# Reordering the first chunks of an FNet and gated-MLP kernel: one early high part moved up, the statistics and norms of four rows spread over more chunks

## The chip, the cores and the metric

The kernel runs on one core of a Trainium2 chip. The metric is the device time of one execution in microseconds. A core has several engines that run their own instruction streams in program order and wait for each other through semaphores: TensorE (PE in the profile, with its weight loads shown apart as PEld), VectorE (DVE), ScalarE (ACT), GpSimd (POOL) and SyncE (SP), which here only issues transfers between the device memory and the on-chip memory. Transfers are carried out by 16 DMA engines.

## The reference

The kernel computes one transformer-like block on x, 2048 rows of 512. Only the first lines matter here:

```python
x = A_x
mod = (_silu(c) @ w_mod).reshape(c.shape[0], 6, 1, -1)
sa, ca, ga, sb, cb, gb = ...
h = _layernorm(x, axis=-1) * (1 + ca) + sa
x = x + ga * _A_ref(h, A_dft_seq_re, A_dft_seq_im, A_dft_hid_re, A_dft_hid_im)
h = _layernorm(x, axis=-1) * (1 + cb) + sb
x = x + gb * _B_ref(h, B_w_in, B_w_sp, B_b_sp, B_w_out)
```

`_A_ref` is a Fourier mixing: y = C_re (h D_re^T) - C_im (h D_im^T), with C the two 2048 x 2048 sequence matrices and D the two 512 x 512 hidden matrices. The kernel multiplies by the sequence matrices first, so its first work is G = C_re x' and C_im x', with x' the plainly normalised x; scale and shift are folded into later matrices. `_B_ref` is a gated MLP with a 2048 x 2048 spatial matrix. All data are 32-bit floats.

## The kernel before, in words

Every product is made from three matmuls on operands split in two: a high part, which is the value rounded to TensorE's 32-bit format, and a low part, the difference between the value and the high part. ACT makes high parts (a copy into the other type), DVE makes low parts (a subtraction). The three products high-high, high-low and low-high are summed in PSUM.

The first stage, `mm_a` (L513), goes through *chunks* n = 0 to 127. A chunk takes one tile of a sequence matrix, 128 x 512, and one *row* of x', that is 128 of its rows by 512 columns, and does twelve matmuls of 128 x 128 by 128 x 512: four column groups k, three products each. The helper `matmul3` has its three matmuls on L96, L97 and L98; the first six chunks have their own order, all from L524: first the four with both high parts, then the four with the tile's low part, then the four with the row's low part.

Which tile and row a chunk takes at the start: chunks 0 and 1 use row 0, 2 and 3 row 1, 4 row 2, 5 row 3, 6 row 2, 7 row 3 (the list `PAIRED`). From chunk 8 on four rows at a time are used: rows 4 to 7 in chunks 8 to 11 and again in 12 to 15, rows 8 to 11 from chunk 16. So each new row has a latest time.

A tile of a sequence matrix goes through these steps, each of which is an instruction:

- it is a quarter of a block, which SyncE loads (`load` L165, `load_block` L152, `load_half` L157). Two blocks are held. A block's successor is loaded when its last quarter has been turned (inside `prep_hi`);
- `prep_hi(n)` (L252): DVE transposes 32 x 32 squares (`squares`, L190 in the profile, tile `t`), then ACT copies it into the high part `ah` (L269);
- `prep_lo(n)` (L279): DVE subtracts, giving the low part `al` (L290).

A row of x goes through these:

- SyncE loads four rows to a tile (`load_x`, L425);
- statistics: `stats_x` (L436, by `norm` and `stats`) puts two operations on DVE (mean and variance, L104 and L106) and three small ones on POOL (L108, L109, L116), whose results are the norm's scale and bias. Rows 0 to 3 use `stats_first` (L439), with three operations on DVE (L442, L444, L445) and two on POOL (L446, L447);
- `norm_x` (L486): ACT applies scale and bias (L120), tile `xn`; all but the first column, which is one in x' and is set by a POOL memset (L491 for rows above 3);
- `hi_h` (L498): ACT copies it in another order into the high part `hh` (L500). Rows 0 to 3 use `hi_first` (L460), which makes `hh` straight from x (L463) with a one-column copy behind it (L469);
- `lo_h` (L502): DVE subtracts, giving `hl` (L505).

The order of all this is written by hand, and each engine follows it. A prologue of plain calls does the first steps. After it, the loop over n calls `prep(n)`, which is `prep_hi(n + 3)` and `prep_lo(n + 2)` unless these have been done, then `mm_a(n)`, then `run(n)`. `run(n)` calls what `at(n, f, ...)` has hung on chunk n, in the order in which the `at` calls were made. A chunk's number there thus places an instruction in each engine's stream, and every instruction behind it on the same engine waits with it.

Other streams in this stretch: SyncE's loads in order are the blocks, rows of x, the vector c (`load_row`) and parts of w_mod (`load_columns`). Eight semaphores serve the transfers in turn, so each issue waits for the landing of an earlier one.

Of the kernel before, what the change touches and what calls it, by code (L numbers as in the profile page):

```python
# [19 lines left out]
def fnet_gmlp_kernel(  # L20
# [103 lines left out]
    def at(n, f, *a):  # L124
        fill.setdefault(n, []).append((f, a))
# [31 lines left out]
    def load_half(tile_, a, h, engs=(nc.sync,) * 4):  # L157

        v = a.rearrange("(b j) (a s) -> a j b s", j=32, a=4)
        for q in range(4):  # L160
            engs[q].dma_start(tile_[32 * q:32 * q + 32], v[q][:, :, 64 * h:64 * h + 64])
# [3 lines left out]
    def load(b):  # L165
        if b < len(src):
            stage[b] = blocks.tile([P, 16, P], F32, tag="stage", bufs=2, name=f"stage{b}")
            load_block(stage[b], src[b])
        elif b < len(src) + 2:
            j = b - len(src)  # L170
            XB.append(blocks.tile([P, 4, Q], F32, tag="stage", bufs=2, name=f"xb{j}"))
            for g in range(2):
                nc.sync.dma_start(XB[j][:, 2 * g:2 * g + 2], ht_d[g].rearrange("(k p) t -> p k t", p=P)[:, 2 * j:2 * j + 2])
                for kk in range(2):
                    TT[2 * j + kk, g] = XB[j][:, 2 * g + kk]
        elif 4 * (b - NB0) < NE - N4:
            i, gh = divmod(b - NB0, NQ)
            g, h = divmod(gh, 2)
            p = PROD[i]
            stage[b] = blocks.tile([P, 2, 16, 64], F32, tag="stage", bufs=2, name=f"stage{b}")  # L180
            for r in range(2):
                load_half(stage[b][:, r], s_d[S_OF[p], r, g] if p in S_OF else
                          quad(w_sp, r + (2 if p == 4 else 0), g + (2 if p == 1 else 0)), h)
# [5 lines left out]
    def squares(dst, block, k):  # L189
        nc.vector.transpose(dst.rearrange("p (b i) -> p b i", i=32), block[:, :, 32 * k:32 * k + 32])  # L190
# [10 lines left out]
    def slot(i, name, dtype=F32):  # L201
        return slots[0].tile([P, Q], dtype, tag=f"slot{i}", bufs=1, name=name)
# [19 lines left out]
    def form_t(n):  # L222

        if n < N1:
            gg, p, kk = (n - N2) // 4, (n - N2) // 2 % 2, n % 2
            return TT[2 * p + kk, gg]
        p = YPROD[(n - N1) // 4 % len(YPROD)]
        gg, kk = divmod(n % 4, 2)
        a, b, c, d = TT[kk, gg], TT[2 + kk, gg], TT[kk, 2 + gg], TT[2 + kk, 2 + gg]
        return {6: S2[gg, kk], 7: a if n < N3 else c, 4: b if n < N3 else d, 5: c if n < N3 else a, 3: d if n < N3 else b}[p]  # L230
# [21 lines left out]
    def prep_hi(n):  # L252
        if n >= NE or n in highs:
            return
        highs.add(n)
        if N2 <= n < N4:
            T[n] = form_t(n)
        else:
            b, k = PAIRED[n] if n < 8 else divmod(n, 4) if n < N2 else (NB0 + (n - N4) // 4, (n - N4) % 4)
            if b != NB0:  # L260
                T[n] = blocks.tile([P, Q], F32, tag="t", bufs=2, name=f"t{n}")
            if b == NB0:
                assert n in T
            elif n >= N4:
                squares(T[n], stage[b][:, k % 2], k // 2)
            else:
                squares(T[n], stage[b], k)
        AH[n] = SE[2][:, n - N4] if N4 <= n < N4 + 4 else blocks.tile([P, Q], F32R, tag="ah", bufs=4, name=f"ah{n}")
        nc.scalar.activation(AH[n], T[n], AF.Copy)  # L269
        if not N2 <= n < N4 and k == 3:  # L270
            done = stage.pop(b)
            if b == 0:
                stage[2] = done
                load_half(done[:, :, 64:], src[2], 1)
            elif b != NB0:
                load(b + 2)


    def prep_lo(n):  # L279
        if n >= NE or n in lows:  # L280
            return
        lows.add(n)
        if N2 <= n < N4 and n % 4 == 3:
            AL[n] = slot(0, f"al{n}", F32R) if slots else zrow[0].tile([P, Q], F32R, tag="z1u", bufs=6, name=f"al{n}")
        elif N4 <= n < N4 + 4:
            AL[n] = slot(9 + n - N4, f"al{n}", F32R)
        else:
            AL[n] = blocks.tile([P, Q], F32R, tag="al", bufs=3, name=f"al{n}")
        t = T.pop(n)
        nc.vector.tensor_tensor(AL[n], t, AH[n].bitcast(F32), op=ALU.subtract)  # L290
# [148 lines left out]
    def stats_first(s):  # L439

        m = spool.tile([P, 12], F32, tag="first", bufs=4, name=f"first{s}")
        nc.vector.bn_stats(m[:, :6], X[s])  # L442
        mv = m[:, 8:]
        nc.vector.bn_aggr(mv[:, :2], m[:, :6])  # L444
        nc.vector.tensor_scalar(mv[:, 1:2], mv[:, 1:2], EPS, None, op0=ALU.add)  # L445
        nc.gpsimd.tensor_tensor(mv[:, 2:3], mv[:, 1:2], mhalf, op=ALU.pow)  # L446
        nc.gpsimd.tensor_scalar(mv[:, 3:4], mv[:, 0:1], mv[:, 2:3], -1.0, op0=ALU.mult, op1=ALU.mult)  # L447
        NRM[s] = mv[:, 2:3], mv[:, 3:4]
# [11 lines left out]
    def hi_first(s):  # L460
        h_hi[s] = hpool.tile([P, ND, P], F32R, name=f"hh{s}")
        h = h_hi[s].rearrange("p k (a i) -> p k a i", i=32)
        nc.scalar.activation(h, X[s].rearrange("p (a k i) -> p k a i", a=4, i=32), AF.Identity,  # L463
                             bias=NRM[s][1], scale=NRM[s][0])
        if s:
            one_first(s)

    def one_first(s):
        nc.scalar.activation(h_hi[s][:, 0, :1], ones[:, :1], AF.Copy)  # L469
# [608 lines left out]
    prep_hi(1)  # L1078
    stats_first(1)
    prep_lo(1)  # L1080
    hi_first(1)
    prep_hi(2)
    load_half(stage[0][:, :, :64], src[2], 0)
    stats_first(2)
    norm_x(1)
# [9 lines left out]
    at(1, lo_h, 2)  # L1095
    at(2, hi_first, 3)
    at(2, norm_x, 3)
    at(2, prep_lo, 5)
    at(3, lo_h, 3)
    at(3, prep_lo, 6)  # L1100
    at(0, load_x, 1, range(2, 4))
    at(2, load_row)
    at(9, silu_row)
# [3 lines left out]
    at(12, load_columns, 0)  # L1107
    at(19, load_ht, 0)
    at(28, load_ht, 1)
    for s, n in ((4, 3), (5, 3), (6, 6), (7, 6), (8, 10), (9, 10)):  # L1110
        m = n + (s == 9)
        at(n, stats_x, s)
        at(m + 1, norm_x, s)
        at(m + 2, hi_h, s)
        at(m + 3, lo_h, s)
# [19 lines left out]
    for j, turn, weigh, row, fold, hi in ((0, (25, 26, 27, 28), (29, 29, 30, 30), 26, (34, 34, 35, 36), (40, 37, 38, 39)),  # L1135
# [8 lines left out]
        n = weigh[3] + 1  # L1144
# [20 lines left out]
    for t in range(NQ):  # L1165
        n = 8 * NQ * (t + 1)
# [136 lines left out]
    for i, p in enumerate(PROD):  # L1303
        for k in range(8):
            n = NB[p] + 2 * k
# [11 lines left out]
    for f in range(NF):  # L1317
        n = N4 + 24 + 8 * f
# [109 lines left out]
```

## Time and profile before

| what | value |
|---|---|
| median of three runs | 933.23 us (933.17 to 933.29) |
| profiled execution | 933.75 us, its span from first to last instruction 932.0 us |
| TensorE busy | 924.7 us, 4053 matmuls |
| VectorE, ScalarE, GpSimd busy | 737.6, 409.3 and 198.3 us |
| granted TensorE clock | 1.000 |

Times in the timeline are from the start of the span. A row of the timeline has the start, the duration, the engine, the line, the operation, what is written from what is read, the shape and how many instructions are merged; in brackets stands how long the engine had been idle and what ended that, as far as semaphores tell. TensorE's matmuls overlap, so the time of one is best read from the distance between starts. For DVE and ACT too, the next instruction can start before the end shown of the one ahead of it.

### The profile page before, as it was taken

The numbers are of one execution on the slowest core, as the hardware profiler recorded it, in microseconds if no ns is written. First come the engines' busy times: TensorE is split into PE (matmuls) and PEld (weight loads), VectorE is DVE, ScalarE is ACT, GpSimd is POOL, SyncE is SP. The second block draws the span as 40 slices with busy tenths as digits, with TensorE's granted clock in tenths as the row PEclk, the third lists the DMA queues.
The fourth block names the chain that finished last, engine by engine and source line by source line (L and its number), as shares of the span: only waits on it lengthen the run. The fifth ranks groups of instructions, "written<-read, shape, count | busy, mean of one in ns | idle before, by whom it ended". The sixth has DMA issues, their size and how long they took to land.

```text
span 932.0 us, 12356 instructions
## 1 busy us (share of the span) xinstructions
PE 924.7 (99%) x4053; PEld 760.3 (82%) x4053; DVE 737.6 (79%) x1217; ACT 409.3 (44%) x734; POOL 198.3 (21%) x376
## 2 busy tenths in 40 slices
PE   8999999999999999999999999999999999999998
PEld 6788888888888888888888888888888888888886
DVE  6889967788687677875669788899799789896762
ACT  5685434233132321322577877674544544331221
POOL 1330000224654165323512320331000000000000
PEclk9999999999999999999999999999999999999999
DMA  9996762856639977996463864444464556744551
GB/s 215 202 225 132 154 155 50 192 147 161 164 84 308 302 210 220 273 331 245 128 224 135 271 208 103 114 107 106 105 145 103 132 140 138 176 100 151 187 175 57
DMA packets 251200, 157.88 MB, mean 169 GB/s; under 512 B 148704, under 2 KB 218592, under 8 KB 251008
## 3 DMA queue, kind: packets, MB, share of 16 engines
q1 hardware_dynamic: 236512, 119.44, 51.7%
q0 software_dynamic: 12272, 36.86, 11.4%
q10 hardware_dynamic: 2352, 0.79, 0.3%
q8 instruction: 32, 0.52, 0.3%
q14 instruction: 32, 0.26, 0.1%
HBM read 120.33 MB, written 36.71 MB: 169 GB/s over the span
## 4 chain that ended last, share of the span: by engine, by line
PE 94%; DMA 2%; DVE 1%; SPq 1%; issue 1%; ACT 0%; ACTq 0%; DVEq 0%
PE gp L98 12%; PE gp L97 11%; PE gp L96 11%; PE gw L98 9%; PE gw L97 9%; PE gw L96 9%; PE yp L98 3%; PE yp L97 3%; PE yp L96 3%; PE op L98 3%; PE op L96 3%; PE op L97 3%; PE fp L98 1%; PE fp L96 1%; PE fp L97 1%; PE z2s L98 1%
## 5 line engine op out<-in xcount | busy, mean ns | idle before, releaser
L269 ACT ACTIVATE ah<-t 128x512 fp32r<-128x512 f32 x236 | 149.0, 631 | 364.7 <-DVE t L190 259.1
L290 DVE TENSOR_TENSOR al<-t,ah 128x512 fp32r<-128x512 f32 x236 | 161.0, 682 | 54.9 <-PE gp L97 25.1
L97 PE MATMUL gp<-al,hh 128*128 128x512 f32 x488 | 190.1, 390 | 0.6 <-DVE al L290 0.6
L98 PE MATMUL gp<-ah,hl 128*128 128x512 f32 x488 | 190.0, 389 | 0.1
L96 PE MATMUL gp<-ah,hh 128*128 128x512 f32 x488 | 190.0, 389 | 0.0
L190 DVE STREAM_TRANSPOSE t<-stage 128x512 f32<-128x512 f32 x236 | 165.7, 702 | 9.6 <-DMA stage<-in_A_dft_seq_re_dram 4.7
L97 PE MATMUL gw<-al,bh 128*128 128x512 f32 x400 | 155.6, 389 | 0.0
L98 PE MATMUL gw<-ah,bl 128*128 128x512 f32 x384 | 149.6, 390 | 0.1
L96 PE MATMUL gw<-ah,bh 128*128 128x512 f32 x384 | 149.4, 389 | 0.0
L97 PEld LDWEIGHTS gp<-al,hh 128*128 128x128 f32 x488 | 91.6, 188 | 20.6 <-DVE al L290 1.6
L98 PEld LDWEIGHTS gp<-ah,hl 128*128 128x128 f32 x488 | 91.6, 188 | 19.4 <-DVE hl L505 0.5
L96 PEld LDWEIGHTS gp<-ah,hh 128*128 128x128 f32 x488 | 91.6, 188 | 19.3 <-ACT hh L500 0.3
L97 PEld LDWEIGHTS gw<-al,bh 128*128 128x128 f32 x400 | 75.1, 188 | 15.7
L98 PEld LDWEIGHTS gw<-ah,bl 128*128 128x128 f32 x384 | 72.1, 188 | 15.6 <-DVE bl L923 0.8
L96 PEld LDWEIGHTS gw<-ah,bh 128*128 128x128 f32 x384 | 72.1, 188 | 14.9
L895 POOL DMA_DIRECT2D s_d<-sj x64 | 35.1, 549 | 108.2 <-DVE sj L887 82.5
L96 PE MATMUL yp<-hth,gh 128*128 128x512 f32 x128 | 49.8, 389 | 0.0
L97 PE MATMUL yp<-htl,gh 128*128 128x512 f32 x128 | 49.8, 389 | 0.0
L98 PE MATMUL yp<-hth,gl 128*128 128x512 f32 x128 | 49.8, 389 | 0.0
L640 POOL DMA_DIRECT2D ht_d<-hturn x62 | 41.0, 667 | 22.2 <-DVE hturn L636 18.3
L96 PE MATMUL op<-woh,uh 128*128 128x512 f32 x112 | 43.6, 389 | 0.0
L97 PE MATMUL op<-wol,uh 128*128 128x512 f32 x112 | 43.6, 389 | 0.0
(233 smaller groups left out, 1455.4 us busy)
## 6 DMA issues: line engine op xcount, KB each, us to landing
sj<-in_B_w_sp_dram SPq DMA_DIRECT2D x32, 512.0 KB, 6.9
s_d<-sj POOLq DMA_DIRECT2D x64, 256.0 KB, 4.2
stage<-s_d SPq DMA_DIRECT2D x128, 128.0 KB, 2.9
stage<-in_A_dft_seq_im_dram SPq DMA_DIRECT2D x60, 256.0 KB, 5.4
stage<-in_A_dft_seq_re_dram SPq DMA_DIRECT2D x56, 256.0 KB, 5.3
stage<-in_B_w_sp_dram SPq DMA_DIRECT2D x88, 128.0 KB, 3.1
wm<-in_w_mod_dram SPq DMA_DIRECT2D x16, 256.0 KB, 6.2
xr<-in_A_x_dram POOLq DMA_DIRECT2D x16, 256.0 KB, 4.7
```

The source lines that it names most:

```text
L96: nc.tensor.matmul(acc, ah, bh, start=first, stop=False, skip_group_check=go_on)
L97: nc.tensor.matmul(acc, ah, bl, start=False, stop=False, skip_group_check=go_on)
L98: nc.tensor.matmul(acc, al, bh, start=False, stop=last, skip_group_check=go_on)
L190: nc.vector.transpose(dst.rearrange("p (b i) -> p b i", i=32), block[:, :, 32 * k:32 * k + 32])
L269: nc.scalar.activation(AH[n], T[n], AF.Copy)
L290: nc.vector.tensor_tensor(AL[n], t, AH[n].bitcast(F32), op=ALU.subtract)
L640: eng.dma_start(v[a, i], ht[32 * a:32 * a + 32].rearrange("c (b r) -> c b r", r=32))
L895: nc.gpsimd.dma_start(s_d[m, r, g][b * P:(b + 1) * P, :], a)
```

## The change

Two things in the order by hand are changed; no instruction is added, removed or altered.

- In the prologue `prep_hi(2)`, which makes the transposed tile and the high part of chunk 2, stands ahead of `hi_first(1)`, which makes row 1's high part, instead of behind it.
- The steps of rows 4 to 7 (statistics, norm, high part, low part) were hung in pairs: both rows of a pair on the same chunk. Now each row has its own chunks. The table gives the chunk to which each step is hung, before and after.

| row | statistics | norm | high part | low part |
|---|---|---|---|---|
| 4 | 3, now 2 | 4, now 3 | 5, now 4 | 6, now 5 |
| 5 | 3, now 3 | 4, now 4 | 5, now 5 | 6, now 6 |
| 6 | 6, now 5 | 7, now 6 | 8, now 7 | 9, now 8 |
| 7 | 6, now 6 | 7, now 7 | 8, now 8 | 9, now 9 |

Within a chunk the order differs as well: rows 4's and 5's statistics now stand ahead of that chunk's other DVE work (low parts of a row and of a tile), where before they stood behind it. Rows 8 and 9 keep their places.

```diff
     prep_hi(1)
     stats_first(1)
     prep_lo(1)
+    prep_hi(2)
     hi_first(1)
-    prep_hi(2)
     load_half(stage[0][:, :, :64], src[2], 0)
     stats_first(2)
     norm_x(1)
...
     at(1, lo_h, 2)
     at(2, hi_first, 3)
     at(2, norm_x, 3)
+    at(2, stats_x, 4)
     at(2, prep_lo, 5)
+    at(3, stats_x, 5)
     at(3, lo_h, 3)
     at(3, prep_lo, 6)
+    at(3, norm_x, 4)
+    at(4, norm_x, 5)
+    at(4, hi_h, 4)
+    at(5, lo_h, 4)
+    at(5, hi_h, 5)
+    at(6, lo_h, 5)
     at(0, load_x, 1, range(2, 4))
...
-    for s, n in ((4, 3), (5, 3), (6, 6), (7, 6), (8, 10), (9, 10)):
+    for s, n in ((6, 5), (7, 6), (8, 10), (9, 10)):
         m = n + (s == 9)
         at(n, stats_x, s)
         at(m + 1, norm_x, s)
         at(m + 2, hi_h, s)
         at(m + 3, lo_h, s)
```

## The prediction

> **What bounds the kernel now.** I read the page's first part, then busy time by windows, then the timeline of each engine over the first 46 us.
>
> ```profile
> span 932.0 us, 12356 instructions
> ...
> PE 924.7 (99%) x4053; PEld 760.3 (82%) x4053; DVE 737.6 (79%) x1217; ACT 409.3 (44%) x734; POOL 198.3 (21%) x376
> ```
>
> TensorE is busy for all but 7.3 us. The same by windows (span, then busy time of PE, PEld, DVE, ACT, POOL, granted clock, DMA share and GB/s):
>
> ```profile
> 40.33:113.00 72.67, 72.67 (x322) 60.19 (x321) 65.21 (x112) 45.28 (x97) 14.09 (x42) 1.00 0.91 175
> ```
>
> From 40.33 us on nothing is left to win: PE is busy for 72.67 of 72.67 us, at full clock. What the change can touch are the chunks before that. A chunk (one call of `mm_a`) is twelve matmuls. Timeline of PE (start, duration, line, idle time in brackets): the last four matmuls of chunk 1, the first of chunks 2, 5 and 6, a wait in chunk 9, the first of chunks 11 and 12:
>
> ```profile
> 12.38 1.08 PE L524 MATMUL gp<-ah,hl 128*128 128x512 f32 x4
> 13.71 1.20 PE L524 MATMUL gp<-ah,hh 128*128 128x512 f32 x4 [0.25 <-ACT ah L269]
> ...
> 22.11 1.20 PE L524 MATMUL gp<-ah,hh 128*128 128x512 f32 x4
> ...
> 24.99 0.40 PE L96 MATMUL gp<-ah,hh 128*128 128x512 f32 x1
> ...
> 34.45 0.50 PE L97 MATMUL gp<-al,hh 128*128 128x512 f32 x1 [0.61 <-DVE al L290]
> 34.79 0.39 PE L98 MATMUL gp<-ah,hl 128*128 128x512 f32 x1
> ...
> 40.33 0.39 PE L96 MATMUL gp<-ah,hh 128*128 128x512 f32 x1
> ...
> 43.05 0.39 PE L96 MATMUL gp<-ah,hh 128*128 128x512 f32 x1
> ```
>
> A chunk without waits takes 43.05 - 40.33 = 2.72 us, 0.227 a matmul. After a wait the next matmul comes 0.34 later instead (34.45 to 34.79): a restart costs 0.11 beside the wait. Chunks 6 to 10 take 40.33 - 24.99 = 15.34 us against 5 x 2.72 = 13.60: **1.74 us of waits**, the longest in chunk 9 for its low part (al). Chunk 2, due at 12.38 + 4 x 0.227 = 13.29, waits until 13.71 for its high part (ah). That is the stock from which the change can draw; no other engine's idle time counts.
>
> **Part 1: ah of chunk 2 ahead of row 1's high part.** Only ACT's order changes. ACT, then DVE:
>
> ```profile
> 12.09 0.81 ACT L463 ACTIVATE hh<-x,first 128x512 fp32r<-128x512 f32 x1 [1.73 <-DMA stage<-in_A_dft_seq_re_dram]
> 12.94 0.20 ACT L469 ACTIVATE hh<-ones 128x1 fp32r<-128x1 f32 x1
> 13.05 0.61 ACT L269 ACTIVATE ah<-t 128x512 fp32r<-128x512 f32 x1
> 13.57 0.80 ACT L120 ACTIVATE xn<-x,first 128x511 f32<-128x511 f32 x1
> 15.82 0.63 ACT L269 ACTIVATE ah<-t 128x512 fp32r<-128x512 f32 x1 [1.45 <-DVE t L190]
> ```
>
> ```profile
> 11.20 0.71 DVE L190 STREAM_TRANSPOSE t<-stage 128x512 f32<-128x512 f32 x1
> 11.83 0.65 DVE L442 BATCH_NORM_STATS2 first<-x 128x6 f32<-128x512 f32 x1
> ...
> 14.47 0.69 DVE L505 TENSOR_TENSOR hl<-xn,hh 128x512 fp32r<-128x512 f32 x1
> 15.08 0.70 DVE L190 STREAM_TRANSPOSE t<-stage 128x512 f32<-128x512 f32 x1
> ```
>
> Steps taken from starts in these rows: transpose to its ah 0.74 (15.08 to 15.82), ah to the next ACT operation 0.52, hh to its one-column copy 0.85, that to the next 0.11, xn to hl 0.90, hl to the next on DVE 0.61. New order: ah 11.20 + 0.74 = 11.94 (in the gap in which ACT waits), hh 12.46, column 13.31, xn 13.42, hl 14.32, transpose 14.93, ah of chunk 3 15.67. So ah moves up by 1.1 us, but hh moves back by 0.37 and the chain behind xn gains only 0.15. Matmuls start 0.66 after ah (13.05 to 13.71) and, from chunk 5, 0.86 after hh (21.25, below, to 22.11). Chunk 2: 12.46 + 0.86 = 13.32 instead of 13.71. Chunk 3 is due 0.11 + 2.72 later, 16.15, and waits for ah until 15.67 + 0.66 = 16.33. Chunk 4: 16.33 + 0.11 + 2.72 = 19.16; chunk 5 due 21.88. Here 0.15 us is won, no more.
>
> **Part 2: statistics of rows 4 and 5.** Row 4's go from behind chunk 3 to behind chunk 2, ahead of al of chunk 5; row 5's stay behind chunk 3 but ahead of hl of row 3 and al of chunk 6. DVE today:
>
> ```profile
> 19.91 0.70 DVE L190 STREAM_TRANSPOSE t<-stage 128x512 f32<-128x512 f32 x1
> 21.38 0.69 DVE L290 TENSOR_TENSOR al<-t,ah 128x512 fp32r<-128x512 f32 x1 [0.76 <-ACT ah L269]
> ...
> 23.10 0.69 DVE L505 TENSOR_TENSOR hl<-xn,hh 128x512 fp32r<-128x512 f32 x1 [0.41 <-ACT xn L120]
> ...
> 24.31 0.69 DVE L104 BATCH_NORM_STATS2 bstx<-x 128x6 f32<-128x512 f32 x1
> ...
> 25.93 0.68 DVE L190 STREAM_TRANSPOSE t<-stage 128x512 f32<-128x512 f32 x1
> ```
>
> The statistics of both rows hold DVE from 24.31 to 25.93, 1.62 us ahead of chunk 7's transpose, 0.81 a row. Two gaps lie earlier: 0.76 and 0.41. With the shift of 0.15: transpose 19.76, statistics of row 4 at 20.39 (0.63 as from 11.20 to 11.83), free 21.20; al of chunk 5 still waits for ACT until 21.23. **Row 4's statistics are free**, covered by that wait; without it they'd cost 0.8. Transpose 21.84, row 5's statistics 22.47, free 23.27. That is past 22.95, when hl of row 3 could start: it starts 0.32 later, at 23.27, ready for PE 0.74 on at 24.01. PE starts chunk 5 at 21.10 + 0.86 = 21.96 and its restart, and reaches the hl group eight matmuls (1.81) later at 23.88: a **new wait of 0.13** and a restart. Chunk 6 starts at 24.01 + 0.11 + 4 x 0.227 = 25.03, against 24.99: all that part 1 won is gone by here. Behind hl, al of chunk 6 is at 23.88 and has half a microsecond to spare.
>
> The rows' transfer must have landed by 20.39 (timeline of SyncE; time to landing of these four issues):
>
> ```profile
> 13.09 1.90 SPq L432 DMA_DIRECT2D x<-in_A_x_dram  x4
> ```
>
> ```profile
> DMA to landing us min/median/max: 3.4/3.5/3.6
> ```
>
> All four are issued by 14.99, so landed by 14.99 + 3.6 = 18.6: 1.8 us to spare.
>
> **Part 3: chunks 6 to 10.** ACT, DVE and POOL of today:
>
> ```profile
> 21.25 0.81 ACT L463 ACTIVATE hh<-x,first 128x512 fp32r<-128x512 f32 x1
> ...
> 22.90 0.62 ACT L269 ACTIVATE ah<-t 128x512 fp32r<-128x512 f32 x1
> 26.70 0.63 ACT L269 ACTIVATE ah<-t 128x512 fp32r<-128x512 f32 x1 [3.17 <-DVE t L190]
> 27.23 0.80 ACT L120 ACTIVATE xn<-x,nmrx,rsx 128x511 f32<-128x511 f32 x1
> ```
>
> ```profile
> 27.36 0.69 DVE L290 TENSOR_TENSOR al<-t,ah 128x512 fp32r<-128x512 f32 x1 [0.17 <-ACT ah L269]
> ```
>
> ```profile
> 25.30 0.19 POOL L108 TENSOR_SCALAR mvx<-mvx 128x1 f32<-128x1 f32 x1 [5.13 <-DVE mvx L106]
> 25.58 0.55 POOL L109 TENSOR_TENSOR rsx<-mvx,mhalf 128x1 f32<-128x1 f32 x1
> 26.23 0.27 POOL L116 TENSOR_SCALAR nmrx<-mvx,rsx 128x1 f32<-128x1 f32 x1
> ```
>
> - Chunk 7: its transpose starts at 24.49 instead of 25.93; the two statistics no longer stand before it. Row 4's norm now stands ahead of ah on ACT. It needs POOL's three operations, over 2.19 after the statistics start (24.31 to 26.50): 20.39 + 2.19 = 22.58, before ACT is through with ah of chunk 6 (22.75 + 0.53 = 23.28). So it runs in a gap of ACT (3.17 today). Its one-column memset now stands behind row 5's operations on POOL, at about 24.9; only row 4's hh, at 26.5, reads that column. ah at 24.49 + 0.77 = 25.26, al 0.66 later (26.70 to 27.36) at 25.92, ended 26.61; due 25.03 + 2.72 + 0.23 = 27.98. Its wait goes.
> - Row 5's norm and row 4's hh follow on ACT at 25.79 and 26.5; hl of row 4 at 27.15 on DVE, row 6's statistics 27.75, transpose of chunk 9 28.56, al of chunk 8 29.2, ended 29.9; due 25.03 + 5.44 + 0.23 = 30.70. Spare 0.8.
> - hl of row 5 29.8, row 7's statistics 30.4, transpose of chunk 10 31.2, al of chunk 9 31.85, ended 32.5; due 33.42, spare 0.9. Today PE gets it at 34.45. So the **longest wait goes**: DVE has the same work ahead of this al as today, except the two statistics that went into earlier gaps. hl of row 6, for which chunk 10 waits today, is then at about 34.0, due 36.4.
>
> Row 6's four steps each come one chunk earlier than today, row 7's stay. No moved step issues a transfer, so SyncE's order stays; the load of chunk 12's block waits for chunk 7's transpose and is issued 1.4 us sooner. POOL's work is the same, 0.19 + 0.55 + 0.27 = 1.01 us a row. From chunk 11 on PE leads by 1.7 us. Chunk 16's transpose waits for a transfer today and is the first place where the lead could run out:
>
> ```profile
> 48.47 0.71 DVE L190 STREAM_TRANSPOSE t<-stage 128x512 f32<-128x512 f32 x1 [3.17 <-DMA stage<-in_A_dft_seq_re_dram]
> 49.11 0.65 DVE L290 TENSOR_TENSOR al<-t,ah 128x512 fp32r<-128x512 f32 x1
> ```
>
> The al behind it is chunk 15's, ended 49.76; PE reads it at 40.33 + 4 x 2.72 + 0.23 = 51.44, so 1.68 us of lead are covered even if no load comes sooner. If they come 1.4 sooner, as their first issue does, there is room.
>
> **Sum.** Chunk 11 starts at 25.03 + 13.60 = 38.63, not 40.33: **1.70 us won**. The profiled execution took 933.75 us (span 932.0, 1.75 around it), 0.52 above the median of the runs, 933.23; its waits are the same kind, so I subtract from the median: 931.53, taken as **931.5**, 0.18% less. About 0.2% (1.87 us) is what a measurement of this kernel can tell from no change, so this is just inside.
>
> Bounds: with no wait at all from chunk 2 on, 13.29 + 9 x 2.72 = 37.77 for chunk 11, a win of 2.56. On the other side DVE could come up to 1.5 later at the low parts of chunks 8 and 9 than I reckon, which costs 0.7 beyond the spare of 0.8. The forecast's own range is 930.9 to 932.2.
>
> **Rivals.**
> 1. *The first chunks wait less than I charge.* The 0.86 us that I leave are short waits and restarts in chunks 2, 3 and 5. If they vanish, the win is 2.56: 930.7. For it: chunk 2 misses by 0.03 only; against: chunk 3's 0.18 hangs on a whole chain. Chance 0.18.
> 2. *Row 4's statistics wait for their transfer.* Place: DVE before al of chunk 5. For it: transfers fill the DMA engines here; against: the 1.8 us to spare. It costs one for one from 20.4 on, and eats the whole win at 22.1; if the landing took twice its 3.6, 22.2, the time is 933.3. Chance 0.06.
> 3. *POOL's small operations hold up DVE* (slower). Place: the subtractions of chunks 5 to 9. If each of four rows' three operations held DVE for its whole length, 4 x 1.01 = 4.04 us, less the win: 933.23 - 1.70 + 4.04 = 935.6. It decides once over 1.7 is lost on DVE's path. Today's rows: the same POOL operation without and with a subtraction beside it,
>
> ```profile
> 4.92 0.56 POOL L446 TENSOR_TENSOR first<-first,mhalf 128x1 f32<-128x1 f32 x1 [3.82 <-DVE first L445]
> ```
>
> ```profile
> 10.60 0.68 DVE L290 TENSOR_TENSOR al<-t,ah 128x512 fp32r<-128x512 f32 x1
> ```
>
> ```profile
> 10.77 0.93 POOL L446 TENSOR_TENSOR first<-first,mhalf 128x1 f32<-128x1 f32 x1 [4.92 <-DVE first L445]
> ```
>
>    POOL takes 0.37 longer and the subtraction its usual 0.68: POOL is the one that waits, and its results have 0.7 to spare at row 4's norm. Chance 0.14. The Trainium skill, "SBUF — State Buffer", section "SBUF: two separate sides", says that the two engines share a pair of ports, that whichever starts first holds it for its whole instruction, and that the other is blocked; by that rule DVE loses where POOL starts first. By it the time would lie between 931.5 and 935.6, by who starts first. The trace agrees, as far as 10.77 shows the order in which DVE starts first.
>
> **How the numbers follow.** Forecast 0.62, of which I put 0.26 beyond the bound (its range lies around 931.36); rivals 0.18, 0.06, 0.14. Faster 0.26 + 0.18 = 0.44, same 0.36 + 0.06 = 0.42, slower 0.14. The range goes from rival 1's full win, 930.6, to 932.9; it leaves out rival 3 and a little on each side.
>
> **What would show it.** Right: row 4's statistics at about 20.4 with al of chunk 5 not later than 21.4; chunk 7's transpose near 24.5; no PE wait for al in chunks 7 and 9 nor for hl in 10; a short wait for hl in chunk 5; chunk 11 near 38.6. Wrong: chunk 6 later than 25.3, an ACT idle gap before a norm that delays ah, or new PE waits after 40 us.

## The result, and the profile after

The changed kernel takes 931.9 us, the median of 22 executions (931.52 to 933.09), beside 933.3 us (933.12 to 934.1) for the kernel before in the same comparison. The ratio is 0.9986 with a 95% interval of 0.9979 to 0.9992: about 1.4 us less, 0.15%. That is within the 0.2% that counts as no change; the forecast time, 0.18% less, lay there too, though the chances left the side open (0.44 for faster, 0.42 for the same). The executions of the changed kernel spread more: 9 of the 22 lie above 932.0, while 19 of the 22 before lie between 933.1 and 933.5. The profiled execution took 932.28 us.

The first part of the page of the kernel after, and its busy time by windows (columns as in the prediction):

```profile
span 930.5 us, 12356 instructions
...
PE 924.8 (99%) x4053; PEld 761.3 (82%) x4053; DVE 736.6 (79%) x1217; ACT 408.8 (44%) x734; POOL 199.4 (21%) x376
```

```profile
38.54:113.00 74.46, 74.46 (x330) 61.72 (x329) 66.51 (x115) 46.38 (x100) 14.29 (x43) 1.00 0.92 177
```

TensorE does the same 924.8 us of work. The stretch without idle time now begins at 38.54 instead of 40.33. PE's timeline of the kernel after, with the first matmuls of chunks 0, 2, 3 and 5, the low-part group of chunk 5, the first of chunks 6 and 11, and one matmul much later:

```profile
7.46 1.19 PE L524 MATMUL gp<-ah,hh 128*128 128x512 f32 x4
...
13.25 1.20 PE L524 MATMUL gp<-ah,hh 128*128 128x512 f32 x4
...
16.27 1.19 PE L524 MATMUL gp<-ah,hh 128*128 128x512 f32 x4
...
21.88 1.20 PE L524 MATMUL gp<-ah,hh 128*128 128x512 f32 x4
22.91 1.07 PE L524 MATMUL gp<-al,hh 128*128 128x512 f32 x4
23.90 1.20 PE L524 MATMUL gp<-ah,hl 128*128 128x512 f32 x4
24.93 0.39 PE L96 MATMUL gp<-ah,hh 128*128 128x512 f32 x1
...
38.54 0.39 PE L96 MATMUL gp<-ah,hh 128*128 128x512 f32 x1
...
807.20 0.50 PE L98 MATMUL gw<-ah,bl 128*128 128x512 f32 x1 [0.37 <-DVE bl L923]
```

Chunks 6 to 10 take 38.54 - 24.93 = 13.61 us, five chunks of 2.72 without a wait. In the execution before they took 15.34. Chunk 0 started at 7.54 before and at 7.46 here; that start moves from one execution to the next with the first transfers (7.32 to 7.73 over all runs shown), so kernels are compared below by the time from chunk 0 to chunk 11: 32.79 before, 31.08 after, **1.71 us less**.

The chain that carries this, on DVE of the kernel after: row 4's statistics, al of chunk 5, row 5's statistics, hl of row 3, chunk 7's transpose and its al, and the al of chunks 8 and 9:

```profile
20.32 0.65 DVE L104 BATCH_NORM_STATS2 bstx<-x 128x6 f32<-128x512 f32 x1
...
21.15 0.69 DVE L290 TENSOR_TENSOR al<-t,ah 128x512 fp32r<-128x512 f32 x1
...
22.39 0.65 DVE L104 BATCH_NORM_STATS2 bstx<-x 128x6 f32<-128x512 f32 x1
...
23.17 0.67 DVE L505 TENSOR_TENSOR hl<-xn,hh 128x512 fp32r<-128x512 f32 x1
...
24.36 1.30 DVE L190 STREAM_TRANSPOSE t<-stage 128x512 f32<-128x512 f32 x2
25.83 0.69 DVE L290 TENSOR_TENSOR al<-t,ah 128x512 fp32r<-128x512 f32 x1 [0.17 <-ACT ah L269]
...
29.09 0.65 DVE L290 TENSOR_TENSOR al<-t,ah 128x512 fp32r<-128x512 f32 x1
...
31.79 0.65 DVE L290 TENSOR_TENSOR al<-t,ah 128x512 fp32r<-128x512 f32 x1
```

Row 4's statistics now stand wholly in time in which DVE had been idle. Row 5's take the other gap of 0.41 and push hl of row 3 back by about 0.3. The al of chunk 9 is ready at 32.44, 0.88 ahead of its matmul at 24.93 + 3 x 2.72 + 0.23 = 33.32; before, PE got it at 34.45.

In the profiled execution the lead of 1.79 (1.71, and 0.08 from chunk 0's start) ends as 1.5 of span (932.0 to 930.5). Most of the difference is the wait at 807.20, for a low part `bl` of the gated MLP: its matmul was due at 806.45 + 0.22 = 806.67, so it waits 0.53 and pays a restart of 0.11. In the execution before the same matmul waited 0.22 and a restart. 0.64 - 0.33 = 0.31 us of the lead go there.

### The profile page after: what moved, and what is told of

Read it like the earlier page. It is cut to its first block, busy times and chain, and to the rows that moved or that the text cites. A ratio compares the mean times of both kernels' runs of the same rounds, so it can differ in the third digit from the quotient of the medians.

```text
span 930.5 us, 12356 instructions
## 1 busy us (share of the span) xinstructions
PE 924.8 (99%) x4053; PEld 761.3 (82%) x4053; DVE 736.6 (79%) x1217; ACT 408.8 (44%) x734; POOL 199.4 (21%) x376
## 4 chain that ended last, share of the span: by engine, by line
PE 98%; DVE 1%; SPq 0%; DMA 0%; issue 0%; ACT 0%; DVEq 0%
PE gp L97 12%; PE gp L98 12%; PE gp L96 12%; PE gw L98 9%; PE gw L97 9%; PE gw L96 9%; PE yp L97 3%; PE yp L96 3%; PE yp L98 3%; PE op L98 3%; PE op L96 3%; PE op L97 3%; PE gp L524 2%; PE fp L97 1%; PE fp L98 1%; PE fp L96 1%
```

## The experiments

All kernels compute the whole block; two do some unused work besides, which is said there. Each median is compared with the kernel before in the same batch (933.28 to 933.45). The second column is how much sooner chunk 11 starts after chunk 0 than in the kernel before, by the profile.

| kernel | lead at chunk 11, us | median, us | ratio to before, 95% |
|---|---|---|---|
| after | 1.71 | 931.90 | 0.9986 (0.9979 to 0.9992) |
| p1_only | 0.15 | 933.27 | 1.0000 (0.9991 to 1.0009) |
| p2_only | 1.56 | 932.10 | 0.9987 (0.9978 to 0.9995) |
| rows45 | 1.70 | 931.77 | 0.9981 (0.9973 to 0.9990) |
| hl_first | 1.75 | 931.68 | 0.9984 (0.9975 to 0.9992) |
| pool_more | 1.68 | 931.69 | 0.9985 (0.9976 to 0.9994) |
| after_z1 | 1.72 | 931.87 | 0.9985 (0.9976 to 0.9994) |
| after_late | 1.71 | 931.61 | 0.9981 (0.9972 to 0.9990) |
| before_late | 0.02 | 933.41 | 0.9999 (0.9990 to 1.0008) |
| extra_load | 1.70 | 933.03 | 0.9996 (0.9987 to 1.0005) |
| after_cols | 1.70 | 933.81 | 1.0006 (0.9997 to 1.0014) |
| best_b | 2.35 | 931.19 | 0.9977 (0.9967 to 0.9986) |
| best_d | 2.35 | 932.27 | 0.9986 (0.9977 to 0.9995) |

### The two parts alone

p1_only is the kernel before with the prologue's move alone:

```diff
     prep_lo(1)
-    hi_first(1)
     prep_hi(2)
+    hi_first(1)
     load_half(stage[0][:, :, :64], src[2], 0)
```

> Part 1 alone (the high part of chunk 2 ahead of row 1's on ACT; rows 4 to 7 as before). If the win comes from rows 4 to 7's spreading: chunk 2 starts 0.4 us sooner than before (13.3), chunk 6 only 0.15 sooner, the waits of chunks 7, 9 and 10 stay (about 1.7 us from chunk 6 to 11), chunk 11 starts 0.15 to 0.25 sooner and the time falls by 0.1 to 0.3 us. If the early high part were what matters, chunk 11 would start over 1 us sooner.

p2_only is the kernel after with that move undone:

```diff
     prep_lo(1)
-    prep_hi(2)
     hi_first(1)
+    prep_hi(2)
     load_half(stage[0][:, :, :64], src[2], 0)
```

> Part 2 alone (rows 4 to 7 spread; the prologue as before). If the win comes from the spreading: chunk 2 as before at 13.7, the wait for row 3's low part in chunk 5 makes chunk 6 start about 0.15 later than before, chunks 6 to 10 have no wait, chunk 11 starts 1.5 to 1.6 us sooner than before. Time 1.2 to 1.5 us less. If part 1 is needed for the rest, waits for al are seen again in chunks 7 and 9 and chunk 11 starts less than 1 us sooner.

PE's timeline of p1_only: the first matmul of chunk 0, the late one of chunk 9, the first of chunk 11:

```profile
7.39 1.19 PE L524 MATMUL gp<-ah,hh 128*128 128x512 f32 x4 [0.39 <-ACT ah L269]
...
34.15 0.50 PE L97 MATMUL gp<-al,hh 128*128 128x512 f32 x1 [0.61 <-DVE al L290]
...
40.03 0.39 PE L96 MATMUL gp<-ah,hh 128*128 128x512 f32 x1
```

Chunk 11 follows chunk 0 by 32.64, 0.15 sooner than before, and chunk 9's idle time of 0.61 stands as it was: the moved high part alone buys the 0.15 us of part 1 and leaves the time as it was. PE's timeline of p2_only, the first matmul of chunks 0 and 11:

```profile
7.43 1.19 PE L524 MATMUL gp<-ah,hh 128*128 128x512 f32 x4
...
38.66 0.39 PE L96 MATMUL gp<-ah,hh 128*128 128x512 f32 x1
```

Chunk 11 follows chunk 0 by 31.23: the other part alone gives 1.56, and 0.15 + 1.56 is the 1.71 of both. So the spreading of the rows' steps carries it. (The medians say no more than this: the intervals of the two kernels overlap.)

### Which rows' steps matter

rows45 pairs rows 6 and 7 again, as in the kernel before:

```diff
-    for s, n in ((6, 5), (7, 6), (8, 10), (9, 10)):
+    for s, n in ((6, 6), (7, 6), (8, 10), (9, 10)):
```

> The changed kernel with rows 6 and 7 hung in a pair as before; only rows 4 and 5 spread. If the win comes from rows 4 and 5's statistics moving into gaps of DVE ahead of chunk 7's transpose: chunk 11 starts within 0.1 us of the changed kernel's 38.54 and no wait is in chunks 7 to 10, since DVE has the same work ahead of chunk 9's al. If each row's own chunk matters, chunk 9 waits for its al by up to 0.8 us again, or chunk 10 for row 6's low part.

The lead is 1.70, and the time that of the kernel after. So spreading rows 4 and 5 is enough. Rows 6's and 7's statistics stood ahead of a low part for which PE waited too (chunk 9's; from 31.41 on in the kernel before). In rows45 they still stand there, but DVE comes to them at 29.46, 1.95 sooner, and that al is ready in time. What spreading rows 6 and 7 alone would give was not run.

### The new wait in chunk 5

hl_first puts row 5's statistics behind chunk 3's other DVE work, so that hl of row 3 needn't wait for them:

```diff
-    at(3, stats_x, 5)
     at(3, lo_h, 3)
     at(3, prep_lo, 6)
+    at(3, stats_x, 5)
```

> The changed kernel with row 5's statistics put behind row 3's low part and chunk 6's low part. If that order is what makes the wait of 0.07 and its restart of 0.11 in chunk 5: both go, chunk 6 starts near 24.75 and chunk 11 near 38.36, 1.96 sooner than before; row 4's low part comes up to 0.7 later and chunk 8's al keeps at least 0.1 to spare, so no new wait. If the wait has another cause it stays, and chunk 8's al may be late by some tenths.

PE's timeline of hl_first: the first matmul of chunk 6, three in chunk 8, the first of chunk 11:

```profile
24.61 0.39 PE L96 MATMUL gp<-ah,hh 128*128 128x512 f32 x1
...
30.05 0.39 PE L96 MATMUL gp<-ah,hh 128*128 128x512 f32 x1
30.28 0.49 PE L97 MATMUL gp<-al,hh 128*128 128x512 f32 x1
30.61 0.40 PE L98 MATMUL gp<-ah,hl 128*128 128x512 f32 x1
...
38.36 0.39 PE L96 MATMUL gp<-ah,hh 128*128 128x512 f32 x1
```

Chunk 6 comes 17.29 us after chunk 0 (7.32 in this execution) instead of 17.47: the wait for hl and its restart are gone, 0.18. But the statistics now stand before the tiles, and al of chunk 8 becomes ready at 30.21, just as PE wants it: the matmul at 30.28 starts on time, yet the next comes 0.33 later instead of 0.23. Chunks 6 to 10 take 13.75 instead of 13.61. So 0.14 of the 0.18 is given back, and my expectation that no other wait would come was wrong.

### POOL's operations beside DVE's subtractions

pool_more gives POOL three more operations for each of rows 4 to 7, written to spare columns that nothing reads:

```diff
     def stats_x(s):
         NRM[s] = norm([X[s]], "x")
+        if 4 <= s <= 7:
+            for i in range(3):
+                spare = spool.tile([P, 1], F32, tag="spare", bufs=4, name=f"spare{s}_{i}")
+                nc.gpsimd.tensor_tensor(spare, NRM[s][0], mhalf, op=ALU.mult)
```

> The changed kernel with three more small operations on POOL behind the statistics of each of rows 4 to 7 (results unused), about 0.2 to 0.6 us each, so POOL's work a row nearly doubles. If POOL's operations do not hold up DVE and their results have time to spare: chunk 11 starts within 0.3 us of the changed kernel's 38.54, time within 0.3 us. If POOL holds DVE up (the slower rival), DVE's subtractions start later by up to the added time and chunk 11 starts 1 to 3 us later, with waits for al in chunks 7 to 9.

POOL's timeline of pool_more around rows 4 and 6, and DVE's al of chunk 8 with the instruction behind it:

```profile
23.04 0.48 POOL L441 TENSOR_TENSOR spare<-rsx,mhalf 128x1 f32<-128x1 f32 x3
...
29.16 0.55 POOL L109 TENSOR_TENSOR rsx<-mvx,mhalf 128x1 f32<-128x1 f32 x1
29.80 0.81 POOL L116 TENSOR_SCALAR nmrx<-mvx,rsx 128x1 f32<-128x1 f32 x1
```

```profile
29.30 0.65 DVE L290 TENSOR_TENSOR al<-t,ah 128x512 fp32r<-128x512 f32 x1
29.88 0.68 DVE L509 TENSOR_TENSOR hl<-xn,hh 128x512 fp32r<-128x512 f32 x1
```

The added operations run for 0.48 us a row, 1.9 us in all; the lead falls by 0.03 and the median not at all. Where the two meet, POOL's operation gets longer (0.81 for one that took 0.27 before) and the subtraction keeps its 0.65. That holds too where POOL's record starts first: its operation at 29.16 is under way when the subtraction starts at 29.30, and the next DVE instruction follows 0.58 later as ever. The Trainium skill, "SBUF — State Buffer", section "SBUF: two separate sides", says that a DVE operation with two inputs in SBUF and a GpSimd operation that reads SBUF need the same pair of ports, and that whichever starts first holds it for its whole instruction while the other is blocked. The trace agrees where DVE starts first (the 0.81). No run here shows DVE blocked by an operation of one column, and there the measurement decides; but the profile itself calls spans on POOL rough, so for how long POOL held the ports at 29.16 is not shown.

### The wait at 807 us

after_z1 issues the two transfers ahead of that low part through POOL's queue, so that SyncE's queue is clear of them:

```diff
-        nc.sync.dma_start(z[:, :f1 - f0], z1_d[t][f0:f1].rearrange("f p t -> p f t"))
+        eng = nc.gpsimd if (p, r) in ((4, 0), (7, 0)) else nc.sync
+        eng.dma_start(z[:, :f1 - f0], z1_d[t][f0:f1].rearrange("f p t -> p f t"))
...
-                nc.sync.dma_start(z[32 * a:32 * a + 32, 3].rearrange("p (b s) -> p b s", s=32), v[a])
+                eng.dma_start(z[32 * a:32 * a + 32, 3].rearrange("p (b s) -> p b s", s=32), v[a])
```

> The changed kernel with the first two loads of the MLP's first half (z1t, issued at about 787 us) on POOL's queue instead of SyncE's, so that the block behind them is not queued behind their landing. If part of the win is given back there: the wait of 0.53 and its restart at 807 us go, the lead over the kernel before is the same at 830 us as at 100, and the median falls by 0.2 to 0.6 us. If not, nothing moves at 807 or the wait goes with the time the same.

The wait is absent in its profile, and the median is 931.87, that of the kernel after. It is absent as well in the profiles of p2_only, pool_more, hl_first, rows45 and after_late, which leave those transfers alone. So it comes in some executions only: it accounts for 0.31 us in the profiled one, and in the median of after_z1 nothing of it shows.

### Where else the lead meets something late: 101 us

The first place that I had named was chunk 16's transpose at 48 us. But DVE has a second tight place, at chunk 34: it folds the weights there. DVE's timeline of the kernel before and then of the kernel after: chunk 34's al and the transpose ahead of it, which is chunk 35's; for the kernel after also the first two instructions of the fold:

```profile
101.16 0.69 DVE L190 STREAM_TRANSPOSE t<-stage 128x512 f32<-128x512 f32 x1
101.77 0.65 DVE L290 TENSOR_TENSOR al<-t,ah 128x512 fp32r<-128x512 f32 x1
```

```profile
98.28 0.70 DVE L387 STREAM_TRANSPOSE acc<-acc 128x512 f32<-128x512 f32 x1
99.02 0.69 DVE L388 TENSOR_REDUCE acc<-acc 128x16 f32<-128x512 f32 x1
...
99.65 0.69 DVE L190 STREAM_TRANSPOSE t<-stage 128x512 f32<-128x512 f32 x1
100.26 0.65 DVE L290 TENSOR_TENSOR al<-t,ah 128x512 fp32r<-128x512 f32 x1
```

PE wants this al at the start of chunk 11 + 23 x 2.72 + 0.23: 103.12 before, 101.33 after. It is ready at 102.42 and 100.91. So PE is 1.79 sooner, DVE 1.51, and the spare time falls from 0.70 to 0.42. In the profiles of p2_only and pool_more, whose leads are no larger (1.56 and 1.68), it did not hold. PE's timeline of p2_only:

```profile
102.02 0.50 PE L97 MATMUL gp<-al,hh 128*128 128x512 f32 x1 [0.41 <-DVE al L290]
```

Due at 38.66 + 62.56 + 0.23 = 101.45, it waits 0.57 and a restart; in pool_more's profile it waits 0.31. after_late takes the fold's instructions ahead of it away, by doing the fold (`split_acc` and what follows) two chunks later; before_late does the same to the kernel before:

```diff
-        n = weigh[3] + 1
+        n = weigh[3] + (3 if j == 0 else 1)
         at(n, split_acc, j)
```

> The changed kernel with the transposed sum of the first hidden matrix's weighted rows (split_acc, about 1.3 us on DVE ahead of chunk 34's low part) and the two steps behind it two chunks later. If part of the win is given back at chunk 34, because DVE is held by late transfers from 47 us on and has no time to spare there: chunk 34's low part has about 1.3 us more to spare (1.7 where the changed kernel's profile has 0.42), no wait there in any profile, and the median falls by 0.1 to 0.3 us to 931.6 to 931.8 with fewer runs above 932.3. If the loss is elsewhere, the median stays at 931.9.

> Control: the kernel before with the later transposed sum of after_late. If that move only pays because the change's lead runs into chunk 34: no difference here, 933.2 to 933.5 us, since chunk 34's low part has 0.7 us to spare in the kernel before and no wait stands there. If the move is a gain of its own, it takes 0.2 to 0.4 us off here too.

In after_late the al is ready 1.97 us before PE wants it. The kernel before does not change with the fold moved (933.41), as its PE had no wait there. The changed kernel's median goes to 931.61, and 10 of its 11 executions lie between 931.46 and 931.85. That is 0.3 us better than the kernel after, in the direction in which the lead would be kept, but within the intervals. Three kernels that leave the fold in its place have medians nearly as low (hl_first 931.68, pool_more 931.69, rows45 931.77), and pool_more's even with the wait at chunk 34 in its profile. So what chunk 34 costs in the median is not shown.

### Transfers ahead of chunk 16

SyncE's timeline of the kernel before and of the kernel after, by issues (start, time over which the four were issued); the first is chunk 12's block, the fourth chunk 16's:

```profile
26.63 2.47 SPq L155 DMA_DIRECT2D stage<-in_A_dft_seq_im_dram  x4
29.20 1.86 SPq L432 DMA_DIRECT2D x<-in_A_x_dram  x4
31.11 3.70 SPq L155 DMA_DIRECT2D wb<-in_w_mod_dram  x4
35.31 6.98 SPq L155 DMA_DIRECT2D stage<-in_A_dft_seq_re_dram  x4
```

```profile
25.10 3.44 SPq L155 DMA_DIRECT2D stage<-in_A_dft_seq_im_dram  x4
28.64 1.86 SPq L432 DMA_DIRECT2D x<-in_A_x_dram  x4
30.54 3.47 SPq L155 DMA_DIRECT2D wb<-in_w_mod_dram  x4
34.51 7.01 SPq L155 DMA_DIRECT2D stage<-in_A_dft_seq_re_dram  x4
```

Chunk 12's block is issued 1.53 sooner, but the four issues then take 3.44 instead of 2.47, and by chunk 16's block 0.80 is left. Further on the profile names landings that this queue waits for: w_mod's parts wait for chunk 12's block (up to 0.8 us before and 0.7 after), and chunk 16's first issue for rows of x (0.4 in both). For the 3.44 it names none. DVE's timeline after:

```profile
47.65 0.71 DVE L190 STREAM_TRANSPOSE t<-stage 128x512 f32<-128x512 f32 x1 [3.32 <-DMA stage<-in_A_dft_seq_re_dram]
48.28 0.65 DVE L290 TENSOR_TENSOR al<-t,ah 128x512 fp32r<-128x512 f32 x1
```

The transpose comes 0.82 sooner (48.47 before), and chunk 15's al has 49.65 - 48.93 = 0.72 to spare instead of 1.68. To see whether this is the next limit, extra_load adds a transfer of 256 KB that nothing uses ahead of chunk 16's block, and after_cols moves a part of w_mod, four transfers, from ahead of that block to behind it, with the work on it later:

```diff
     at(5, load_columns, 1)
+    def load_extra():
+        spare = rows.tile([P, D], F32, tag="row", bufs=6, name="spare")
+        nc.sync.dma_start(spare, x[:P, :])
+
+    at(5, load_extra)
     at(8, load_x, 3)
```

> The changed kernel with one transfer more (256 KB of x, not used) on SyncE's queue ahead of chunk 16's block. If transfers set the time of chunks 15 to 34: chunk 11 starts as in the changed kernel (38.5), that block's last quarter lands about 1.2 us later (near 48.7), chunk 15 waits for its low part by about 0.5 us or chunk 34 by up to 0.8, and the time rises by 0.5 to 1.0 us. If DVE's own work sets it, no wait appears and the time stays.

```diff
-    at(5, load_columns, 1)
     at(8, load_x, 3)
+    at(8, load_columns, 1)
...
-    for j, ns in ((1, (12, 14, 17, 18)), (0, (21, 22, 23, 24))):
+    for j, ns in ((1, (16, 17, 18, 19)), (0, (21, 22, 23, 24))):
```

> The changed kernel with the 1 MB of w_mod's first quadrant (load_columns(1)) loaded behind the next block and the next rows of x instead of ahead of them, and its weighing three to four chunks later. If transfers set the time of chunks 15 to 34: chunk 16's block lands 4 to 5 us sooner, DVE's idle time of 3.3 us at 47 goes, the low part of chunk 15 has 3 us or more to spare and chunk 34's 1 us or more; median 931.5 to 931.8, fewer slow runs. If not, or if the late weighing holds up DVE in chunks 16 to 20, the time stays or rises.

PE's timeline of extra_load, chunk 15's matmul that takes al, and DVE's, its transpose of chunk 16:

```profile
50.54 0.50 PE L97 MATMUL gp<-al,hh 128*128 128x512 f32 x1 [0.69 <-DVE al L290]
```

```profile
49.20 0.71 DVE L190 STREAM_TRANSPOSE t<-stage 128x512 f32<-128x512 f32 x1 [4.21 <-DMA stage<-in_A_dft_seq_re_dram]
```

One transfer more makes the transpose 1.55 later; PE then waits 0.86 and a restart in chunk 15, and 0.30 and a restart in chunk 34, and the median is 933.03, 1.1 more than after and a little beyond the 0.5 to 1.0 expected. So the next limit behind the lead is this landing, 0.7 us away. The opposite edit did not help, though. PE's timeline of after_cols, and two rows of DVE's:

```profile
103.30 0.50 PE L97 MATMUL gp<-al,hh 128*128 128x512 f32 x1 [1.35 <-DVE al L290]
```

```profile
46.63 0.69 DVE L290 TENSOR_TENSOR al<-t,ah 128x512 fp32r<-128x512 f32 x1 [0.81 <-PE gp L97]
...
69.15 0.17 DVE L364 TENSOR_SCALAR cols<-cols 128x4 f32<-128x4 f32 x1 [2.03 <-ACT wt L360]
```

The block now lands at 42.6, and chunk 15's al has 4.9 us to spare. But DVE cannot run ahead with it: it waits for PE to release a buffer of `al`. The work on w_mod comes later: a step of it at 63.90, which the kernel after has earlier, puts DVE 1.1 us behind the kernel after, and at 69.15 DVE has waited 2.03 us for ACT's part of that work, where it waited 0.82 in the kernel after. From there it stays 2.3 behind as far as the fold (100.62 against 98.28). PE waits 0.22 and a restart at 79.70, and 1.51 and a restart in chunk 34. The median is 933.81, no better than before. I had expected 931.5 to 931.8: freeing the transfers alone did not help, because DVE could not make up for the later work. In the kernel after it is busy for 21.3 of the 23 us from 80 to 103 us.

### Versions that might beat both

best_b is the kernel after with chunk 3's transpose and high part ahead of row 1's low part, and with the fold two chunks later as in after_late:

```diff
     prep_lo(2)
-    lo_h(1)
     prep_hi(3)
+    lo_h(1)
     hi_first(2)
...
-        n = weigh[3] + 1
+        n = weigh[3] + (3 if j == 0 else 1)
```

> The changed kernel with chunk 3's transpose and high part ahead of row 1's low part in the prologue, in DVE's gap of 0.84 us there, and the move of after_late. If chunk 3 waits for the chain norm, low part, transpose, high part: its wait of 0.14 and restart go, chunk 5 still waits for row 3's low part behind row 5's statistics, and chunk 11 starts 0.2 to 0.5 us sooner than 38.54, near 38.2. Median 931.2 to 931.6. If ACT's order is the limit instead, chunk 3 waits as before.

best_d is best_b with after_cols' edit added:

```diff
-    at(5, load_columns, 1)
     at(8, load_x, 3)
+    at(8, load_columns, 1)
...
-    for j, ns in ((1, (12, 14, 17, 18)), (0, (21, 22, 23, 24))):
+    for j, ns in ((1, (16, 17, 18, 19)), (0, (21, 22, 23, 24))):
```

> best_b with the transfer order of after_cols. best_b still waits in chunk 15 (0.1 and a restart), where its longer lead meets the same landing. If the transfer is the cause, that wait goes and the median is 930.8 to 931.1, 2.3 to 2.6 below the kernel before; if it is not, the median stays at 931.2.

PE's timeline of best_b: the first matmul of chunks 0 and 11, and one in chunk 15:

```profile
7.73 1.20 PE L524 MATMUL gp<-ah,hh 128*128 128x512 f32 x4 [1.08 <-ACT ah L269]
...
38.17 0.39 PE L96 MATMUL gp<-ah,hh 128*128 128x512 f32 x1
...
49.38 0.50 PE L97 MATMUL gp<-al,hh 128*128 128x512 f32 x1
```

Chunk 3's wait is gone and chunk 11 follows chunk 0 by 30.44: a lead of 2.35. Chunk 15's al was due at 38.17 + 10.88 + 0.23 = 49.28, so 0.10 of wait and a restart are paid there: the landing of chunk 16's block is now met. The median of 931.19 is the lowest of all kernels here, 2.3 us below the kernel before in its batch. best_d frees that landing and has the shortest profiled execution (930.94), but its executions spread from there to 933.43 and its median is 932.27; the expectation was wrong. What its longer executions wait for was not seen, since only the one was profiled.

## Why the prediction was right, and where it was not

**What bounds it, and part 1.** Right. ah of chunk 2 was reckoned at 11.94 and came at 11.86; chunk 2 started at 13.25 (13.32 reckoned) and chunk 3 at 16.27 (16.33); the whole prologue lay 0.08 earlier. That only 0.15 us is won there is shown by p1_only.

**Part 2.** Right, the new wait included. Row 4's statistics ran at 20.32 (20.39 reckoned) in DVE's wait for ACT, al of chunk 5 at 21.15 (21.23). hl of row 3 came late by 0.08 and a restart: 23.90 against 22.91 + 4 x 0.227 = 23.82 (0.13 reckoned). Chunk 6 started at 24.93 (25.03).

**Part 3.** Right. Chunk 7's transpose at 24.36 (24.49), its al at 25.83 (25.92); the al of chunks 8 and 9 have 0.87 and 0.88 to spare (0.8 and 0.9). No wait is left in chunks 6 to 10, and rows45 shows that spreading the steps of rows 4 and 5 is enough for that.

**The sum.** 1.70 us reckoned at chunk 11, 1.71 measured. Between the medians there are 1.4, and the prediction of 931.5 is 0.4 below the 931.9. The lead's full 1.7 lies inside the ratio's interval (1 - 1.71 / 933.3 = 0.9982), so the 0.3 is not itself established; that the executions spread further up is. That the time fell inside 0.2% is luck rather than merit, since the sum lay 0.02% from that bound. "From 40.33 us on nothing is left to win" rested on the window up to 113 us: the same execution loses 0.33 us at 808 us.

**The step that was mis-sized** is the end of part 3, "If they come 1.4 sooner, as their first issue does, there is room". The first issue did come 1.53 sooner, but the landing for chunk 16 only 0.82, since the four issues of chunk 12's block took 0.97 longer and the ones behind it waited for landings as before. The spare time at chunk 15 fell to 0.72: the lead was still covered there, with less than half of the room. And chunk 16 was not the tightest place on the way: chunk 34's al, which the prediction did not look at, had 0.70 to spare before the change, less than the lead of 1.7, and only because DVE itself came 1.51 sooner did it hold in the profiled execution. In p2_only and pool_more it cost 0.57 and 0.31 with restarts, and at 807 us the profiled execution itself loses 0.31. The prediction names "new PE waits after 40 us" as a sign of being wrong, but puts no price on them. Which of them make up the longer of the 22 executions stays open: executions that are only timed leave no trace.

**The rivals.** The first did not come: the waits of chunks 3 and 5 stood. best_b shows that the stock was there, with a lead of 2.35 of the 2.56 named once chunk 3's wait is removed. The second did not come: DVE began row 4's statistics without a wait for a transfer. The third falls with pool_more: 1.9 us more of POOL's work left the time from chunk 0 to chunk 11 where it was, to 0.03.

## What to carry to other kernels

Small operations cost nothing only in a gap of their engine: look for the gap that ends in a wait for another engine, and put them there. When the bounding engine gains a lead, compare the lead with the spare time of every later operand it takes, far past the change, and not with the first one alone; an issue that comes sooner need not land sooner. An operation moved up in a stream moves back whatever it passes, so price both: 1.1 us sooner for one high part was 0.15 for the chain.

## What was not expected of the hardware

A matmul that takes an operand just as it becomes ready can still cost a restart: in hl_first the one at 30.28 was on time, 0.07 after its al was ready, and the next came 0.33 later instead of 0.23. POOL's operations of one column grow beside a DVE subtraction (from 0.27 to 0.81) while the subtraction is not held up, also in the case where POOL's record starts first. And 256 KB more ahead of a block made its transpose 1.55 us later (47.65 to 49.20), while issuing the queue 1.53 us sooner brought it forward by only 0.82. From 30 to 48 us the DMA share was 1.17 with 224 GB/s, against 1.17 with 228 GB/s in the kernel before, so the sooner issue let no more through there.
